# Decode attention with an MLP branch: keys loaded two heads at a time and transposed in place, output weights in three pieces

## The chip, the cores and the metric

The kernel runs on one core of one Trainium2 chip. The metric is the device time of one execution in microseconds. The kernel before takes 150.57 us (median of 3 runs, 149.56 to 151.60).

## What is computed

One token, x of 576 numbers, goes through two branches, and a scalar gate mixes them:

```python
W = 4096                                   # the last 4096 of 32768 keys
q = (x @ wq)                               # 32 query heads of 128; 16 key/value heads
scores = einsum(q, k[:, :, Sk-W:]) * 128**-0.5
o = einsum(softmax(scores), v[:, :, Sk-W:])
a = o.reshape(1, 4096) @ wo                # 4096 x 576
b = gelu(x @ w1 + b1) @ w2 + b2            # 576 -> 4608 -> 576
g = sigmoid((x * gate_w).sum())
out = g * a + (1 - g) * b
```

All inputs are bf16. The keys and the values in the window are 16.8 MB each, w1 and w2 5.3 MB each, wq and wo 4.7 MB each: 53.6 MB in all.

## The kernel before

All large loads are issued on SyncE's queue (SP) in this order: w1 (L79), wq (L83), keys, first half of w2 (L363), values, wo (L404), second half of w2 (L406). They go into four large buffers by tag, 32 KB per partition or more: w1 and key group 2 and w2 use B; wq, key group 3 and value group 2 use A; key group 0, value group 0 and value group 3 use C; key group 1, value group 1 and wo use D. SP works in program order, and a load into a buffer that is still in use holds every load behind it. So the first half of w2 waits until key group 2 has been transposed, value group 2 until key group 3 has been, value group 3 until TensorE has consumed value group 0, and wo until it has consumed value group 1.

**Keys (L287 to L316).** A group g is four heads. Partition p holds keys (p % 32) * 128 to +127 of head p // 32 of the group, `k_t[p, 128 keys, 128]`. It is loaded in two to four pieces (L280; `k_cuts`), 16 KB a partition for a 2 MB piece, 8 KB for a 1 MB piece: ten loads in all. For each half f (64 keys of each partition) two VectorE transposes (L296) work in 32x32 blocks of 4-byte words (two bf16 numbers as one word). Each takes 128x2048 words. The view `"p (n b k) -> p n k b"` on both sides makes a block's words be read, and written, with a step of 8 words (32 bytes). The result goes to `kt` (two buffers, `kt_pool`). TensorE then multiplies the half: 4 heads by 4 weight sets `qz` (L309), 16 matmuls of 512 columns into one half of `s_ps`. Its moving operand takes every second bf16 in runs of 8 (a step of 4 bytes). All 16 need both transposes. In all: 16 transposes, 128 matmuls.

**Softmax (L319 to L358).** One maximum over `s_ps` (L320), two tiny matmuls that spread it (L322, L334), eight exponentials of 128x512 on ScalarE (L347), which read `s_ps` contiguously, two VectorE transposes of 128x2048 bf16 (L355), contiguous on both sides, then the sums (L369 to L377). The first half of w2 is multiplied meanwhile (L178, L365).

**Values and output (L385 to L423).** 128 small matmuls for each of four value groups (L391), then the output scaling (L409 to L417), 64 matmuls with wo (two for each of 32 rows) and 36 with the second half of w2 (all on L178, two column halves of 288), and the output row (L425). wo comes in two loads, rows 0 to 11 and 12 to 31; the second half of w2 comes in five, the last three of 288, 144 and 144 KB.

Of the kernel before, what the change touches and what calls it, by code (L numbers as in the profile page):

```python
# [8 lines left out]
FP32 = mybir.dt.float32  # L9
BF16 = mybir.dt.bfloat16  # L10
# [6 lines left out]
def kernel(  # L17
# [15 lines left out]
    nc = tc.nc  # L33

    P = 128
    D = 576
    Hq, Hkv, Dh = 32, 16, 128
    Sk, W = 32768, 4096
    HB = 4
    NG = Hkv // HB  # L40
    NKP = P // HB
    NCK = W // NKP
    SL = NCK // 2
# [10 lines left out]
    big = ctx.enter_context(tc.tile_pool(name="big", bufs=1, side="right"))  # L54
# [42 lines left out]
    for t in range(2):  # L97
        nc.vector.tensor_copy(
            out=alt[:, t : NI + 1 : 2], in_=par[:, t : t + 1].to_broadcast([P, (NI + 1) // 2])
# [6 lines left out]
    for i in range(NI):  # L106
        nc.tensor.matmul(  # L107
            xs_ps[:, i : i + 1],
            lhsT=xdup[:, i : 2 * D : NI],
            rhs=one_b[0:1, 0:1],  # L110
            start=(i == 0),
            stop=(i == NI - 1),
            skip_group_check=True,
        )
    x2 = const.tile([P, NI, 2], BF16, name="x2")
    for t in range(2):
        nc.vector.tensor_tensor(
            out=x2[:, :, t], in0=xs_ps[:], in1=alt[:, t : t + NI], op=ALU.mult
# [13 lines left out]
        out=pen[:], in0=pen[:], scalar1=1e30, scalar2=-1e30, op0=ALU.mult, op1=ALU.add  # L132
# [3 lines left out]
    for j in range(4):  # L136
# [6 lines left out]
        out=junk_row,  # L143
# [17 lines left out]
        out=omg[:], in0=g_t[:], scalar1=-1.0, scalar2=1.0, op0=ALU.mult, op1=ALU.add  # L161
# [3 lines left out]
        out=b2g[:], in0=b2_row, scalar1=omg[0:1, 0:1], scalar2=None, op0=ALU.mult  # L165
# [3 lines left out]
        out=gh[:, 0, :], in0=hi4[:], scalar1=g_t[:, 0:1], scalar2=None, op0=ALU.mult  # L169
# [21 lines left out]
    for j in range(NJ):  # L191
        nc.tensor.matmul(
            h_ps[:, j:NF:NJ],
            lhsT=b1_t[:, j:FH:NJ],
            rhs=ident[0:2, 0:2],
            start=(j == 0),
            stop=False,
            skip_group_check=True,
# [3 lines left out]
    for i in range(NI):  # L202
        for j in range(NJ):
            nc.tensor.matmul(  # L204
                h_ps[:, j:NF:NJ],
                lhsT=w1_t[:, i, j:FH:NJ],
                rhs=x2[:, i, :],
                start=False,
                stop=(i == NI - 1 and j == NJ - 1),
                skip_group_check=True,  # L210
# [8 lines left out]
        out=poly[:],  # L219
# [20 lines left out]
    for i in range(NI):  # L240
        for j in range(Hq // 2):
            nc.tensor.matmul(  # L242
                q_ps[:, j : Hq : Hq // 2],
                lhsT=wq_t[:, i, j * Dh : (j + 1) * Dh],
                rhs=x2[:, i, :],
                start=(i == 0 and j == 0),
                stop=(i == NI - 1 and j == Hq // 2 - 1),
                skip_group_check=True,
# [4 lines left out]
    for j in range(4):  # L253
        nc.tensor.matmul(
            qj_ps[:, j, :, :].rearrange("p h t -> p (h t)"),
            lhsT=perm[:, j, :, :].rearrange("p b l -> p (b l)"),
            rhs=q_b[:],
            start=True,
            stop=True,
        )  # L260
    for b in range(4):
# [4 lines left out]
            out=diag[:, :, 0:512].rearrange("p h (j m) -> p h j m", m=P)[:, :, :, 0:2],  # L266
            in_=qj_ps[quad].rearrange("p j h t -> p h j t"),
        )
    qz = qz_flat[:, 0 : Hkv * 4 * P].rearrange("p (h j m) -> p h j m", h=Hkv, j=4)


    def head_rows(cache, g):
        src = cache[0, HB * g : HB * g + HB, Sk - W : Sk, :]
        return src.rearrange("b (k c) d -> k b (c d)", k=NKP)

    def load(tile_, cache, g, cuts):
        src = head_rows(cache, g)
        c0 = 0
        for n in cuts:
            nc.sync.dma_start(  # L280
                out=tile_[:, c0 : c0 + n, :].rearrange("p c d -> p (c d)"),
                in_=src[:, :, c0 * Dh : (c0 + n) * Dh],
            )
            c0 += n

    s_ps = ps_s.tile([P, NCK * 8], FP32, name="s_ps")
    k_cuts = ((32, 32, 64), (64, 64), (64, 64), (64, 32, 32))  # L287
    for g in range(NG):
        k_t = big.tile([P, NCK, Dh], BF16, name="k_t", tag="CDBA"[g])
        load(k_t, A_k_cache, g, k_cuts[g])  # L290
        for f in range(2):
            kt = kt_pool.tile([P, SL * Dh], BF16, name="kt", tag="kt")
            for u in range(2):
                half = SL * Dh // 2
                c0 = f * SL + u * SL // 2
                nc.vector.transpose(  # L296
                    out=kt[:, u * half : (u + 1) * half]
                    .bitcast(FP32)
                    .rearrange("p (n b k) -> p n k b", b=HB, k=8),
                    in_=k_t[:, c0 : c0 + SL // 2, :]  # L300
                    .rearrange("p c d -> p (c d)")
                    .bitcast(FP32)
                    .rearrange("p (n k b) -> p n k b", b=HB, k=8),
                )
            kv = kt[:].rearrange("p (c e b k t) -> p c e b k t", e=2, b=HB, k=8, t=2)
            for b in range(HB):
                for j in range(4):
                    h = HB * g + b
                    nc.tensor.matmul(  # L309
                        s_ps[:, f * 512 : (f + 1) * 512].rearrange("p (c k) -> p c k", k=8),  # L310
                        lhsT=qz[:, h, j, :],
                        rhs=kv[:, :, j // 2, b, :, j % 2],
                        start=(h == 0 and j == 0),
                        stop=(h == Hkv - 1 and j == 3),
                        skip_group_check=True,
                    )  # L316


    m1 = const.tile([P, 1], FP32, name="m1")  # L319
# [7 lines left out]
        out=mh4[:],  # L327
# [11 lines left out]
        out=negm[:], in0=pen[:], in1=mb_ps[:].to_broadcast([P, HB]), op=ALU.add  # L339
# [4 lines left out]
    for f in range(2):  # L344
        cs = slice(f * SL, (f + 1) * SL)
        for b in range(HB):
            nc.scalar.activation(  # L347
                out=p_t[:, cs, :, b],
                in_=s_ps[:, f * 512 : (f + 1) * 512].rearrange("p (c k) -> p c k", k=8),
                func=ACT.Exp,  # L350
                bias=negm[:, b : b + 1],
                scale=SCALE,
                accum_out=sums[:, f * HB + b : f * HB + b + 1],
            )
        nc.vector.transpose(  # L355
            out=pt[:, cs, :].rearrange("p c h -> p (c h)"),
            in_=p_t[:, cs, :, :].rearrange("p c k b -> p (c k b)"),
        )  # L358
# [5 lines left out]
    for f in range(NJ):  # L364
# [13 lines left out]
        out=rgh[:],  # L378
# [8 lines left out]
    for g in range(NG):  # L387
        v_t = big.tile([P, NCK, Dh], BF16, name="v_t", tag="CDAC"[g])
        load(v_t, A_v_cache, g, v_cuts[g])
        for c in range(NCK):  # L390
            nc.tensor.matmul(  # L391
                o_ps[:, 8 * g : 8 * g + 8, 0],
                lhsT=v_t[:, c, :],
                rhs=pt[:, c, 8 * g : 8 * g + 8],
                start=(c == 0),
                stop=(c == NCK - 1),
# [3 lines left out]
    RO = Hq * Dh // P  # L400
    wo_t = big.tile([P, RO, D], BF16, name="wo_t", tag="D")
    wo_src = A_wo.rearrange("(p r) n -> p r n", r=RO)
    for r0, r1 in ((0, 12), (12, RO)):
        nc.sync.dma_start(out=wo_t[:, r0:r1, :], in_=wo_src[:, r0:r1, :])  # L404
    for j0, j1 in ((0, 9), (9, 14), (14, 16), (16, 17), (17, 18)):
        nc.sync.dma_start(out=w2_t[:, NJ + j0 : NJ + j1, :], in_=w2_src[:, 1, j0:j1, :])  # L406
# [3 lines left out]
        out=om[:], in0=o_ps[:].to_broadcast([P, Hq, 4]), in1=rgh[:], op=ALU.mult  # L410
# [10 lines left out]
    for f in range(NJ, NF):  # L421
# [5 lines left out]
        out=out.rearrange("a b (s d) -> (a b s) d", s=2), in_=out_row[0:64:32, :]  # L427
# [31 lines left out]
```

## Time and profile before

| what | us |
|---|---|
| median of 3 runs | 150.57 |
| the profiled execution, its own time | 151.29 |
| its span in the profile | 149.5 |
| VectorE busy | 78.7 |
| TensorE busy (modelled) | 85.1 |
| DMA queue of SP: 53.61 MB, share of 16 engines' span | 85.9% |

The profile is of one execution; its span starts with the first instruction and leaves out 1.79 us of the execution's own time. "Busy" is the time in which an engine had at least one instruction running; the DMA share is the mean over 16 DMA engines. PE is TensorE, PEld its weight loads, DVE VectorE, ACT ScalarE, SPq the queue of SyncE. [...]

### The profile page before, as it was taken

What the parts mean: (1) busy time and instruction counts of PE and PEld (TensorE: products, weight loads), DVE (VectorE), ACT (ScalarE), POOL (GpSimd) and SP (SyncE); (2) the same over time, 40 slices, a digit from 0 to 9 for tenths busy, and PEclk for the clock granted to TensorE, in tenths of its full rate; (3) what the DMA queues carried; (4) which work ended last, traced back from release to release, by engine and by line L of the source; (5) the groups of instructions that cost most, each with busy time, mean ns of one, the idle gap of its engine ahead of it and who ended that gap; (6) DMA issues with size and microseconds to landing.
All of it is one profiled execution on the core that took longest, in us unless ns stands there. A gap on an engine that the chain in (4) does not pass through costs nothing.

```text
span 149.5 us, 2460 instructions
## 1 busy us (share of the span) xinstructions
PE 85.1 (57%) x1126; PEld 53.3 (36%) x1126; DVE 78.7 (53%) x81; ACT 11.9 (8%) x21; POOL 0.7 (0%) x6
## 2 busy tenths in 40 slices
PE   0189991700768188909094949550069936361791
PEld 0187991600223022404031313230069936330450
DVE  5990022099999999999999980406350000100001
ACT  3000000010000000000000000099600000000000
POOL 1000000000000000000000000000000000000000
PEclk9999999999999956999969595997555555555579
DMA  5999999999999999950089999999963899999940
GB/s 163 428 429 420 434 431 397 421 445 434 425 421 419 421 434 425 408 237 0 0 277 427 444 438 447 438 460 421 430 298 66 377 403 428 451 437 393 404 158 0
DMA packets 4344, 53.78 MB, mean 360 GB/s; under 512 B 487, under 2 KB 748, under 8 KB 1006
## 3 DMA queue, kind: packets, MB, share of 16 engines
q1 hardware_dynamic: 4324, 53.61, 85.9%
q8 instruction: 9, 0.15, 0.4%
q10 hardware_dynamic: 10, 0.01, 0.0%
q14 instruction: 1, 0.01, 0.0%
HBM read 53.62 MB, written 0.00 MB: 359 GB/s over the span
## 4 chain that ended last, share of the span: by engine, by line
DVE 38%; DMA 33%; PE 15%; ACT 7%; issue 5%; SPq 0%; DVEq 0%; ACTq 0%
DVE kt L296 34%; DMA wo_t<-in_A_wo_dram 14%; DMA wq_t<-in_A_wq_dram 14%; ACT p_t L347 6%; PE y_ps L178 5%; PE o_ps L391 5%; DMA w_t<-in_B_w_dram 4%; PE s_ps L309 4%; DVE pt L355 2%; DVE m L320 1%; PE q_ps L242 1%; PE t_ps L373 0%; DVE qz_flat L265 0%; DVE out_row L425 0%; PE mt_ps L322 0%
## 5 line engine op out<-in xcount | busy, mean ns | idle before, releaser
L296 DVE STREAM_TRANSPOSE kt<-k_t 128x2048 f32<-128x2048 f32 x16 | 58.3, 3776 | 0.0
L309 PE MATMUL s_ps<-kt,qz_flat 128*128 128x512 bf16 x128 | 38.6, 466 | 26.1 <-DVE kt L296 26.1
L309 PEld LDWEIGHTS <-qz_flat 128*128 128x128 bf16 x128 | 14.5, 113 | 49.8 <-issue 39.9
L391 PE MATMUL o_ps<-pt,v_t 128*128 128x8 bf16 x512 | 14.3, 168 | 4.6 <-issue 4.1
L391 PEld LDWEIGHTS <-v_t 128*128 128x128 bf16 x512 | 14.2, 104 | 4.8 <-issue 4.2
L347 ACT ACTIVATE p_t<-s_ps,negm 128x512 bf16<-128x512 f32 x8 | 9.7, 1425 | 66.4 <-DVE negm L338 66.4
L178 PE MATMUL y_ps<-wo_t,ov 128*1 128x288 bf16 x64 | 8.0, 443 | 6.3 <-DMA wo_t<-in_A_wo_dram 6.3
L204 PEld LDWEIGHTS <-w_t 128*128 128x128 bf16 x162 | 10.2, 165 | 1.0 <-issue 1.0
L204 PE MATMUL h_ps<-x,w_t 128*128 128x2 bf16 x162 | 10.4, 202 | 0.0
L409 DVE TENSOR_TENSOR om<-o_ps,rgh 128x128 bf16<-128x128 f32 x1 | 0.3, 291 | 18.0 <-PE o_ps L391 18.0
L425 DVE CAST out_row<-y_ps 33x288 bf16<-33x288 f32 x1 | 0.4, 449 | 16.4 <-PE y_ps L178 16.4
L355 DVE STREAM_TRANSPOSE pt<-p_t 128x2048 bf16<-128x2048 bf16 x2 | 4.6, 2311 | 7.4 <-ACT p_t L347 7.4
L178 PEld LDWEIGHTS <-ov 128*1 128x1 bf16 x64 | 4.0, 122 | 9.9 <-issue 6.3
L373 PE MATMUL t_ps<-ls,ones 128*128 128x32 f32 x2 | 0.6, 398 | 10.8 <-DVE ls L371 10.8
L242 PE MATMUL q_ps<-x,wq_t 128*128 128x2 bf16 x144 | 4.3, 166 | 4.0 <-DMA wq_t<-in_A_wq_dram 4.0
L242 PEld LDWEIGHTS <-wq_t 128*128 128x128 bf16 x144 | 4.1, 104 | 4.2 <-DMA wq_t<-in_A_wq_dram 4.2
L178 PE MATMUL y_ps<-w_t,gt 128*1 128x288 bf16 x72 | 5.3, 289 | 0.0
L213 DVE COPY hacc<-h_ps 128x36 f32<-128x36 f32 x1 | 0.2, 195 | 9.7 <-PE h_ps L204 9.7
L107 PE MATMUL xs_ps<-one_b,rows 1*128 1x1 bf16 x9 | 0.7, 195 | 6.6 <-DVE rows L104 6.6
L373 PEld LDWEIGHTS t_ps<-ls,ones 128*128 128x128 f32 x2 | 0.5, 313 | 11.1 <-issue 11.1
L320 DVE TENSOR_REDUCE m<-s_ps 128x1 f32<-128x1024 f32 x1 | 1.2, 1225 | 5.4 <-PE s_ps L309 5.4
L201 DVE MEMSET qz_flat<- 128x4240 f32 x1 | 3.6, 3592 | 0.9 <-issue 0.9
(66 smaller groups left out, 27.6 us busy)
## 6 DMA issues: line engine op xcount, KB each, us to landing
k_t<-in_A_k_cache_dram SPq DMA_DIRECT2D x6, 2048.0 KB, 31.9
v_t<-in_A_v_cache_dram SPq DMA_DIRECT2D x3, 4096.0 KB, 24.4
w_t<-in_B_w_dram SPq DMA_DIRECT2D x3, 1728.0 KB, 10.4
k_t<-in_A_k_cache_dram SPq DMA_DIRECT2D x4, 1024.0 KB
wo_t<-in_A_wo_dram SPq DMA_DIRECT2D x1, 2880.0 KB
w_t<-in_B_w_dram SPq DMA_DIRECT2D x1, 2592.0 KB
wq_t<-in_A_wq_dram SPq DMA_DIRECT2D x1, 2048.0 KB
v_t<-in_A_v_cache_dram SPq DMA_DIRECT2D x1, 2048.0 KB
```

What stands on the lines that cost most here:

```text
L107: nc.tensor.matmul(xs_ps[:, i : i + 1], lhsT=xdup[:, i : 2 * D : NI], rhs=one_b[0:1, 0:1], start=(i == 0), stop=(i == NI - 1), skip_group_ ...
L178: nc.tensor.matmul(y_ps[32 * s : 32 * s + 1, :], lhsT=vec, rhs=row[:, s * DH : (s + 1) * DH], start=start, stop=stop, skip_group_check=True,)
L201: nc.vector.memset(qz_flat[:].bitcast(FP32), 0.0)
L204: nc.tensor.matmul(h_ps[:, j:NF:NJ], lhsT=w1_t[:, i, j:FH:NJ], rhs=x2[:, i, :], start=False, stop=(i == NI - 1 and j == NJ - 1), skip_grou ...
L242: nc.tensor.matmul(q_ps[:, j : Hq : Hq // 2], lhsT=wq_t[:, i, j * Dh : (j + 1) * Dh], rhs=x2[:, i, :], start=(i == 0 and j == 0), stop=(i ...
L296: nc.vector.transpose(out=kt[:, u * half : (u + 1) * half] .bitcast(FP32) .rearrange("p (n b k) -> p n k b", b=HB, k=8), in_=k_t[:, c0 : c ...
L309: nc.tensor.matmul(s_ps[:, f * 512 : (f + 1) * 512].rearrange("p (c k) -> p c k", k=8), lhsT=qz[:, h, j, :], rhs=kv[:, :, j // 2, b, :, j ...
L320: nc.vector.reduce_max(out=m1[:], in_=s_ps[:], axis=AX.X)
L347: nc.scalar.activation(out=p_t[:, cs, :, b], in_=s_ps[:, f * 512 : (f + 1) * 512].rearrange("p (c k) -> p c k", k=8), func=ACT.Exp, bias=n ...
L355: nc.vector.transpose(out=pt[:, cs, :].rearrange("p c h -> p (c h)"), in_=p_t[:, cs, :, :].rearrange("p c k b -> p (c k b)"),)
L373: nc.tensor.matmul(t_ps[:], lhsT=ones[:], rhs=ls[:], start=True, stop=True)
L391: nc.tensor.matmul(o_ps[:, 8 * g : 8 * g + 8, 0], lhsT=v_t[:, c, :], rhs=pt[:, c, 8 * g : 8 * g + 8], start=(c == 0), stop=(c == NCK - 1),)
```

## The change

Keys are now loaded for two heads at a time. Partition p holds keys (p % 64) * 64 to +63 of head p // 64 of the pair, 16 KB a partition, one 2 MB load for a pair; the first and the last pair come in two loads of 1 MB. The loads are as many and as large as before, in the same place of SP's queue. The two transposes of a pair work on the words as they lie, with a step of one word on both sides. TensorE's moving operand now takes every fourth bf16 in runs of 16 (a step of 8 bytes), and the first 8 of a pair's 16 matmuls need only the first transpose. The keys stand in `s_ps` in another order, so an exponential takes every second fp32 of it (a step of 8 bytes), over both halves. The values are loaded as they were. wo comes in three loads, rows 0 to 11, 12 to 23 and 24 to 31.

```diff
-    k_cuts = ((32, 32, 64), (64, 64), (64, 64), (64, 32, 32))
     for g in range(NG):
-        k_t = big.tile([P, NCK, Dh], BF16, name="k_t", tag="CDBA"[g])
-        load(k_t, A_k_cache, g, k_cuts[g])
+        k_t = big.tile([P, 2, SL, Dh], BF16, name="k_t", tag="CDBA"[g])
         for f in range(2):
+            h0 = HB * g + 2 * f
+            src = A_k_cache[0, h0 : h0 + 2, Sk - W : Sk, :].rearrange(
+                "b (k c) d -> k b (c d)", k=P // 2
+            )
+            n_cut = 2 if h0 in (0, Hkv - 2) else 1
+            n = SL // n_cut
+            for u in range(n_cut):
+                nc.sync.dma_start(
+                    out=k_t[:, f, u * n : (u + 1) * n, :].rearrange("p c d -> p (c d)"),
+                    in_=src[:, :, u * n * Dh : (u + 1) * n * Dh],
+                )
             kt = kt_pool.tile([P, SL * Dh], BF16, name="kt", tag="kt")
             for u in range(2):
                 half = SL * Dh // 2
                 nc.vector.transpose(
-                    out=kt[:, u * half : (u + 1) * half]
-                    .bitcast(FP32)
-                    .rearrange("p (n b k) -> p n k b", b=HB, k=8),
-                    in_=k_t[:, c0 : c0 + SL // 2, :]
+                    out=kt[:, u * half : (u + 1) * half].bitcast(FP32),
+                    in_=k_t[:, f, u * SL // 2 : (u + 1) * SL // 2, :]
                     .rearrange("p c d -> p (c d)")
-                    .bitcast(FP32)
-                    .rearrange("p (n k b) -> p n k b", b=HB, k=8),
+                    .bitcast(FP32),
                 )
-            kv = kt[:].rearrange("p (c e b k t) -> p c e b k t", e=2, b=HB, k=8, t=2)
-            for b in range(HB):
-                for j in range(4):
...
-                        s_ps[:, f * 512 : (f + 1) * 512].rearrange("p (c k) -> p c k", k=8),
-                        rhs=kv[:, :, j // 2, b, :, j % 2],
+            kv = kt[:].rearrange("p (c e k b t) -> p c e k b t", e=2, b=2, k=16, t=2)
+            for u in range(2):
+                for b in range(2):
+                    for j in range(4):
...
+                            s_ps[:, u * 512 : (u + 1) * 512].rearrange("p (c k) -> p c k", k=16),
+                            rhs=kv[:, u * SL // 2 : (u + 1) * SL // 2, j // 2, :, b, j % 2],
...
-                in_=s_ps[:, f * 512 : (f + 1) * 512].rearrange("p (c k) -> p c k", k=8),
+                in_=s_ps[:].rearrange("p (c k u) -> p u c k", k=8, u=2)[:, f],
...
-    for r0, r1 in ((0, 12), (12, RO)):
+    for r0, r1 in ((0, 12), (12, 24), (24, RO)):
```

On TensorE, in the middle of the first 16 key matmuls, the program before reads (a name in brackets is the engine whose semaphore an instruction waits for):

```order
691 L309 MATMUL s_ps<-kt,qz_flat 128x512
692 L309 LDWEIGHTS qz_flat
693 L309 MATMUL s_ps<-kt,qz_flat 128x512
694 L309 LDWEIGHTS qz_flat
695 L309 MATMUL s_ps<-kt,qz_flat 128x512
696 L309 LDWEIGHTS qz_flat
697 L309 MATMUL s_ps<-kt,qz_flat 128x512
```

and now, at the same rows:

```order
691 L316 MATMUL s_ps<-kt,qz_flat 128x512
692 L316 LDWEIGHTS qz_flat
693 L316 MATMUL s_ps<-kt,qz_flat 128x512
694 L316 LDWEIGHTS qz_flat
695 L316 MATMUL s_ps<-kt,qz_flat 128x512 [waits DVE_49]
696 L316 LDWEIGHTS qz_flat
697 L316 MATMUL s_ps<-kt,qz_flat 128x512
```

The ninth matmul of every 16 now has a wait of its own on VectorE; before, only the first of 16 had one, for both transposes.

On SP, from the last value loads to the end, the program before reads (DMAHW0 to DMAHW7 are eight semaphores that the loads take in turn, so a load can wait for the one eight before it):

```order
20 L280 DMA v_t<-in_A_v_cache_dram 128x1x4096 x2
21 L404 DMA wo_t<-in_A_wo_dram 128x6912 [waits DMAHW6_49,PE_49]
22 L404 DMA wo_t<-in_A_wo_dram 128x11520 [waits DMAHW4_49]
23 L406 DMA w_t<-in_B_w_dram 128x5184
24 L406 DMA w_t<-in_B_w_dram 128x2880
25 L406 DMA w_t<-in_B_w_dram 128x1152 [waits DMAHW7_49]
26 L406 DMA w_t<-in_B_w_dram 128x576 [waits DMAHW0_49]
27 L406 DMA w_t<-in_B_w_dram 128x576 [waits DMAHW1_49]
```

and now:

```order
20 L281 DMA v_t<-in_A_v_cache_dram 128x1x4096 x2
21 L411 DMA wo_t<-in_A_wo_dram 128x6912 [waits DMAHW6_49,PE_49]
22 L411 DMA wo_t<-in_A_wo_dram 128x6912 [waits DMAHW4_49]
23 L411 DMA wo_t<-in_A_wo_dram 128x4608
24 L413 DMA w_t<-in_B_w_dram 128x5184
25 L413 DMA w_t<-in_B_w_dram 128x2880 [waits DMAHW7_49]
26 L413 DMA w_t<-in_B_w_dram 128x1152 [waits DMAHW0_49]
27 L413 DMA w_t<-in_B_w_dram 128x576 [waits DMAHW1_49]
28 L413 DMA w_t<-in_B_w_dram 128x576 [waits DMAHW2_49]
```

One more load stands in the queue, and each w2 load behind it takes the semaphore of the next value load: the last of them now waits for the last value load.

## Rows read from the trace of the kernel before

**Rows 1.** The page's part 2: 40 slices of 3.74 us, busy tenths.
```profile
DVE 5990022099999999999999980406350000100001
DMA  5999999999999999950089999999963899999940
```
**Rows 2.** Chain that ended last, in order of time: start us, us, what.
```profile
28.22 1.03 PE q_ps L242 x32
...
30.74 12.30 DVE kt L296 x4
...
74.58 14.47 DVE kt L296 x4
...
89.09 5.32 PE s_ps L309 x16
...
94.43 1.24 DVE m L320
...
110.48 6.82 PE o_ps L391 x256
...
146.36 0.45 DVE out_row L425
```
**Rows 3.** Waits of SP's queue: line, releaser, us in total, times, longest us.
```profile
SPq L280 <- PE o_ps L391: 20.8, 1, 20.8
...
SPq L363 <- DVE kt L296: 16.8, 1, 16.8
```
**Rows 4.** Timeline of SP's queue around two of its waits' ends.
```profile
74.56 0.34 SPq L363 DMA_DIRECT2D w_t<-in_B_w_dram  x1
...
113.91 1.83 SPq L280 DMA_DIRECT2D v_t<-in_A_v_cache_dram  x3
```
**Rows 5.** Stretches: window and us, busy PE, PEld, DVE, ACT, POOL, PEclk, DMA share, GB/s.
```profile
0.00:26.00 26.00, 15.40 (x253) 14.16 (x254) 11.25 (x49) 1.69 (x3) 0.70 (x6) 1.00 0.94 386
4.00:64.00 60.00, 37.31 (x407) 24.01 (x408) 43.00 (x59) 0.92 (x4) 0.00 (x0) 0.94 1.01 425
66.00:74.00 8.00, 3.62 (x16) 1.53 (x16) 8.00 (x3) 0.00 (x0) 0.00 (x0) 1.00 0.02 8
...
78.00:110.00 32.00, 15.77 (x79) 6.52 (x77) 17.82 (x12) 9.68 (x16) 0.00 (x0) 0.77 1.01 433
110.00:118.00 8.00, 8.00 (x290) 8.00 (x291) 0.65 (x2) 0.00 (x0) 0.00 (x0) 0.50 0.52 190
118.00:142.00 24.00, 12.72 (x281) 9.53 (x279) 0.48 (x2) 0.00 (x0) 0.00 (x0) 0.50 1.00 420
```
**Rows 6.** Groups of instructions by line and shape: busy us, mean ns | idle before.
```profile
L296 DVE STREAM_TRANSPOSE kt<-k_t 128x2048 f32<-128x2048 f32 x16 | 58.3, 3776 | 0.0
...
L347 ACT ACTIVATE p_t<-s_ps,negm 128x512 bf16<-128x512 f32 x8 | 9.7, 1425 | 66.4 <-DVE negm L338 66.4
...
L355 DVE STREAM_TRANSPOSE pt<-p_t 128x2048 bf16<-128x2048 bf16 x2 | 4.6, 2311 | 7.4 <-ACT p_t L347 7.4
```
**Rows 7.** TensorE's timeline, two groups of key matmuls.
```profile
45.57 3.62 PE L309 MATMUL s_ps<-kt,qz_flat 128*128 128x512 bf16 x16 [2.06 <-DVE kt L296]
...
89.09 5.30 PE L309 MATMUL s_ps<-kt,qz_flat 128*128 128x512 bf16 x16 [1.95 <-DVE kt L296]
```
**Rows 8.** Groups by line and shape: matmuls whose weights lie 36 bytes apart (L204) and side by side (L242).
```profile
L204 PE MATMUL h_ps<-x,w_t 128*128 128x2 bf16 x162 | 10.4, 202 | 0.0
...
L242 PE MATMUL q_ps<-x,wq_t 128*128 128x2 bf16 x144 | 4.3, 166 | 4.0 <-DMA wq_t<-in_A_wq_dram 4.0
```
**Rows 9.** TensorE's timeline, the end.
```profile
139.09 4.96 PE L178 MATMUL y_ps<-wo_t,ov 128*1 128x288 bf16 x40 [3.86 <-DMA wo_t<-in_A_wo_dram]
143.84 2.47 PE L178 MATMUL y_ps<-w_t,gt 128*1 128x288 bf16 x36
```

More of the change, by code (lines that the diff above doesn't have):

```diff
@@ L294 @@
                 half = SL * Dh // 2
-                c0 = f * SL + u * SL // 2
                 nc.vector.transpose(
-                    out=kt[:, u * half : (u + 1) * half]
-                    .bitcast(FP32)
-                    .rearrange("p (n b k) -> p n k b", b=HB, k=8),
-                    in_=k_t[:, c0 : c0 + SL // 2, :]
+                    out=kt[:, u * half : (u + 1) * half].bitcast(FP32),
+                    in_=k_t[:, f, u * SL // 2 : (u + 1) * SL // 2, :]
                     .rearrange("p c d -> p (c d)")
-                    .bitcast(FP32)
-                    .rearrange("p (n k b) -> p n k b", b=HB, k=8),
-                )
-            kv = kt[:].rearrange("p (c e b k t) -> p c e b k t", e=2, b=HB, k=8, t=2)
-            for b in range(HB):
-                for j in range(4):
-                    h = HB * g + b
-                    nc.tensor.matmul(
-                        s_ps[:, f * 512 : (f + 1) * 512].rearrange("p (c k) -> p c k", k=8),
-                        lhsT=qz[:, h, j, :],
-                        rhs=kv[:, :, j // 2, b, :, j % 2],
[L313 to L316, printed above, removed]
+                    .bitcast(FP32),
+                )
+            kv = kt[:].rearrange("p (c e k b t) -> p c e k b t", e=2, b=2, k=16, t=2)
+            for u in range(2):
+                for b in range(2):
+                    for j in range(4):
+                        h = h0 + b
+                        nc.tensor.matmul(
+                            s_ps[:, u * 512 : (u + 1) * 512].rearrange("p (c k) -> p c k", k=16),
+                            lhsT=qz[:, h, j, :],
+                            rhs=kv[:, u * SL // 2 : (u + 1) * SL // 2, j // 2, :, b, j % 2],
+                            start=(h == 0 and j == 0),
+                            stop=(h == Hkv - 1 and j == 3),
+                            skip_group_check=True,
+                        )
     m1 = const.tile([P, 1], FP32, name="m1")
```

## The prediction

> **What bounds the kernel now.** I read the 40 slices first. DMA is full from the second slice on, except for two holes: slices 18 to 21, and slices 30 and 31 [rows 1]. Through the key stage VectorE is full from 30.7 us to 89 us. The question is why the DMA stops twice, and the chain in order of time and SP's waits answer it. The chain runs through the transposes from 30.74 us until TensorE's last key matmuls start at 89.09 [rows 2]: 16 of them in 58.3 us [rows 6], 3.64 us each, with no wait. SP's longest waits name the holes: the first half of w2 waited 16.8 us for a transpose, and value group 3 waited 20.8 us for TensorE to consume value group 0 [rows 3]. Those loads went out at 74.56 and 113.91 us [rows 4]. The stretches size them: 425 GB/s while keys stream, 8 GB/s from 66 to 74 us, 433 GB/s from 78 to 110, 190 from 110 to 118, 420 after [rows 5]. So VectorE is late with the keys, and its lateness empties the DMA queue twice; everywhere else DMA sets the pace.
>
> **When bytes land.** w1 and wq are 10.03 MB; by 26 us 386 GB/s x 26 us = 10.04 MB had moved [rows 5], and the last of wq released TensorE at 28.2 [rows 2]: a landing comes about 2.1 us behind its bytes. A key pair (2.10 MB) takes 2.10/0.425 = 4.93 us. Key pieces therefore land at 30.6 and 33.0 (1 MB each), then 38.0, 42.9, 47.8, 52.8, 57.7, 62.6 (2 MB), 65.1 and 67.6 (1 MB). The change keeps sizes, row lengths and order of these loads, so I cost them at nothing.
>
> **The transposes.** Sixteen before, sixteen after, of 128x2048 words; what goes is the step of 32 bytes. No row shows a contiguous transpose of 4-byte words. The bounds: 3.64 us each, no gain, and 2.31 us, the contiguous transpose of as many bf16 [rows 6]. Cheaper than that has no row, and since DMA paces the stage below 4.93/2 = 2.46 us, it would bring nothing. I take 2.31, the row equal in form and element count. Two take 4.62 us a pair, less than the 4.93 us in which a pair arrives, so VectorE waits for data: the pairs end at 35.3, 42.6, 47.5, 52.4, 57.4, 62.3 and 67.2, the last pair's halves at 69.5 and 71.8 (against 89.05).
>
> **TensorE in the key stage.** Still 128 matmuls of 512 columns. A group of 16 took 3.62 us, or 5.30 us when it began at the lower clock [rows 7]: 0.226 us each at best. The new step of 8 bytes has no row. [...] The upper bound comes from weight loads: with columns 36 bytes apart a pair of weight load and matmul took 10.4/162 = 64 ns, side by side 4.3/144 = 30 ns [rows 8], a factor of 2.15, so 0.486 us a matmul. I take no cost, because two neighbours 8 bytes apart are nearer to 4 than to 36. Then a pair costs 3.6 us of its 4.93, with pauses under 2 us. After the last transpose 8 matmuls remain instead of 16: 1.8 us, end at 73.6 (against 94.41).
>
> [...]
>
> **Softmax.** From the end of the scores to the first value matmul took 110.48 - 94.41 = 16.1 us [rows 2]; now it would be 73.6 + 16.1 = 89.7. The exponentials read `s_ps` with a step of 8 bytes; nothing before does, and I bound each of the eight (9.7/8 = 1.21 us apart [rows 6]) by no cost and by twice as long, 9.7 us in all. I take none, because the sum hardly feels it (below).
>
> **DMA after the keys.** The first half of w2 can go out at 62.3 instead of 74.56, before the last key bytes have moved at 66 us, so the first hole closes. w2's half and value groups 0 to 2 are 2.65 + 12.58 = 15.24 MB, 35.2 us at 433 GB/s: until 101.2. Value group 3 needs group 0 consumed: 89.7 + 3.4 (half of the 6.82 us of rows 2) = 93.1. That is some 7 us before the queue runs dry (a load's first bytes move about 1 us behind its issue), so the second hole closes too, and this margin is what covers the exponentials. The added wait of the last w2 piece for the last value piece (landed about 113) costs nothing: behind it stands only the output, and it is wanted near 128. Value group 3 takes 4.19/0.433 = 9.7 us, wo and w2's second half 7.37 MB/0.420 = 17.5 us. Last bytes at 101.2 + 9.7 + 17.5 = 128.4.
>
> **The tail.** Before, the last bytes moved at 139.1 - 2.1 + 2.65/0.420 = 143.3 (the last wo landed at 139.1, and w2's 2.65 MB follow it). TensorE began the last 40 wo matmuls at 139.09 (0.119 us each) and ended the 36 of w2 at 146.3 [rows 9], 3.0 us behind the bytes. With three pieces 24 of the 40 are done earlier and 16 remain, 1.9 us; then the last small w2 pieces decide, 2.1 us behind the bytes, and some matmuls: 2.4 us (it could be 2.1 to 3.0). The output takes 149.5 - 146.34 = 3.16 us as before.
>
> **Sum.** 128.4 + 2.4 + 3.16 = 134.0 us of span, plus the 1.79 us around it: 135.8 us, against 151.29 of the same execution before (15.5 less: 14.9 from the two holes, 0.6 from the tail). Against the median of 150.57 the same gain would give 135.1.
>
> **The rivals.**
>
> *TensorE becomes the bound, 146.0.* If the new step doubles a matmul to 0.452 us, the stage ends at 33.0 + 128 x 0.452 = 90.9. The pair whose transposes release w2 waits for its `kt` buffer until 33.0 + 64 x 0.452 = 61.9 and ends at 66.5, so DMA pauses 1.5 us; value group 0 is consumed at 90.9 + 16.1 + 3.4 = 110.4 and group 3 starts 8.7 us late. 135.8 + 10.2 = 146.0. For it: the weight loads' factor. [...] Part of it (up to 0.3 us a matmul) would cost almost nothing.
>
> *The exponentials double, 138.3.* Value group 0 is consumed 9.7 us later, at 102.8; group 3's bytes begin 2.6 us late, at 103.8. Then 135.8 + 2.5 = 138.3. Nothing in the profile speaks for or against, as all its reads of `s_ps` are contiguous. [...]
>
> *The transposes stay at 3.64 us, 148.0.* That is so if words of 4 bytes are slow in themselves, not their step; the two transposes of rows 6 differ in both. Only the shorter ends remain: 8 matmuls instead of 16 (half of 5.30 = 2.7 us, which move group 3's start) and 0.6 in the tail. 151.3 - 3.3 = 148.0.
>
> *Slower: the matmul's step costs more than doubling.* Place: the key matmuls. The point from which it decides: group 0 must be consumed later than 113.9 as now, so 33.0 + 128c + 19.5 > 113.9, c = 0.48 us. The weight loads' factor (0.486) reaches just there. At 0.55 us the group is consumed at 122.9, 9 us later: 151.3 + 9 - 0.6 = 159.7. Against it: that would be worse per column than loads that skip 36 bytes.
>
> **How the numbers follow.** Forecast 0.64, with a range of its own of 133 to 138 (DMA at 433 GB/s to the end, or a tail and a start that are 2 us worse); TensorE as the bound 0.20; exponentials 0.06; unchanged transposes 0.07; slower 0.03. A measurement of this kernel can tell about 2% from no change. Faster: 0.64 + 0.20 + 0.06 and half of the unchanged transposes, which lie on the edge: 0.93. Within 2%: 0.04. Slower: 0.03. The range runs from 133 to 145 us: it takes in the forecast, the doubled exponentials and most of TensorE's slowing, short of full doubling.
>
> **What would show it.** Right: transposes near 2.3 us with waits for key loads before each pair; groups of 8 key matmuls near 1.8 us; scores done near 74 us; no DMA slice under 9 tenths from the second to the last but two; w2's first half issued near 62 us. Wrong: transposes of 3.6 us (the step was not the cause), key matmuls over 0.3 us apart without a wait, an SP wait of value group 3 on TensorE that leaves the DMA empty, or a lower DMA rate in the key stage, for which nothing here speaks.

## The result, and the profile after

The changed kernel takes 145.78 us (median of 4 runs, 145.26 to 145.91) against 150.12 us for the kernel before (median of 4 too): a ratio of 0.969 with a 95% interval of 0.961 to 0.977. It is faster, as forecast, but by 4.3 us and not by 15; the forecast of 135.8 and its range (to 145.0) both miss. The time is that of the rival in which TensorE becomes the bound, 146.0. (Ratios here and below leave out runs over 1.5% slower than the fastest of the same kernel, so one can differ from the quotient of the medians beside it.)

Two things in the description ahead have to be put right. First, the loads have the key block outside the head ("k b (c d)"): before, partition p holds 128 keys of head p % 4; after, it holds 64 keys of head p % 2. Heads alternate from partition to partition. That is why a transposed block of 32 words mixes heads, why the old transposes moved words about, and why the new matmuls step over the other head's words. Second, the old transposes stepped on the writing side alone: the view `"p (n b k) -> p n k b"` stands on `kt`, and the view of `k_t` is `"p (n k b) -> p n k b"`, the words as they lie. No time in the prediction depends on either, but experiment 5 does.

The page's part 2 of the changed kernel, 40 slices of 3.60 us (PEclk is the clock that TensorE was granted, here in tenths of the full one, in the stretches and in [rows 5] as a share of it):

```profile
PE   0189992718999999999999997740099764384391
DVE  5991003068489858393939102205710000100001
...
PEclk9999999999999999999999999867555555559959
DMA  5999999999999999997999999999404999999930
```

VectorE, full from 30.7 to 89 us before [rows 1], now has pauses. TensorE is full instead, from 40 to 89 us, at a granted clock of 1.00. Of the DMA's first hole a dip is left, in slice 19; the second hole is still there, in slices 29 to 31.

The groups of instructions that answer to [rows 6] and [rows 7] (busy us, mean ns of one | idle before, releaser):

```profile
L316 PE MATMUL s_ps<-kt,qz_flat 128*128 128x512 bf16 x128 | 55.6, 609 | 3.6 <-DVE kt L305 3.6
L305 DVE STREAM_TRANSPOSE kt<-k_t 128x2048 f32<-128x2048 f32 x16 | 36.2, 2294 | 12.8 <-PE s_ps L316 9.2
...
L354 ACT ACTIVATE p_t<-s_ps,negm 128x512 bf16<-128x512 f32 x8 | 9.7, 1411 | 60.9 <-DVE negm L345 60.9
```

The transposes take 2.29 us instead of 3.78, as forecast, and now wait 9.2 us for TensorE to free `kt`; the exponentials take the same 9.7 us with their new step. The matmuls have grown. The chain that ended last, in order of time, says how much (start us, us, what):

```profile
37.97 2.32 DVE kt L305
...
40.34 48.52 PE s_ps L316 x112
...
88.88 1.24 DVE m L327
...
104.92 6.82 PE o_ps L398 x256
...
136.61 4.06 PE y_ps L178 x36
...
140.69 0.45 DVE out_row L432
```

112 matmuls run back to back for 48.5 us: 0.433 us each, against 0.226 in [rows 7]. The scores are done at 88.9 instead of 94.4, and that is all that is left of the 21 us by which they were to come sooner. The waits of SP's queue (us in total, times, longest) show what follows, against [rows 3]:

```profile
SPq L281 <- PE o_ps L398: 23.8, 1, 23.8
...
SPq L370 <- DVE kt L305: 8.2, 1, 8.2
```

The first half of w2 waits only 8.2 us for its transpose, but value group 3 waits longer than before for value group 0 to be consumed. The loads go out at these times (compare [rows 4]), and the stretches give the price (window and us, busy PE, PEld, DVE, ACT, POOL, PEclk, DMA share, GB/s):

```profile
65.79 0.34 SPq L370 DMA_DIRECT2D w_t<-in_B_w_dram  x1
...
108.35 1.83 SPq L281 DMA_DIRECT2D v_t<-in_A_v_cache_dram  x3
```

```profile
63.00:66.00 3.00, 3.00 (x8) 0.80 (x7) 2.76 (x2) 0.00 (x0) 0.00 (x0) 1.00 0.84 350
66.00:70.00 4.00, 4.00 (x10) 1.03 (x9) 1.84 (x1) 0.00 (x0) 0.00 (x0) 1.00 0.87 289
66.00:101.00 35.00, 27.15 (x93) 8.12 (x91) 13.20 (x9) 9.17 (x15) 0.00 (x0) 0.93 1.00 421
101.00:118.00 17.00, 11.46 (x410) 11.43 (x411) 3.25 (x5) 0.51 (x2) 0.00 (x0) 0.50 0.56 228
```

From 63 to 70 us the DMA falls short of 421 GB/s by (1 - 350/421) x 3 + (1 - 289/421) x 4 = 1.8 us: that is left of the first hole, as the first half of w2 goes out at 65.8. From 101 to 118 it moves 228 GB/s: (1 - 228/421) x 17 = 7.8 us lost, because value group 3 may not be loaded before 108.4.

### The profile page after: what moved, and what is told of

Its sections match the earlier page's. It is cut to its first block, busy times and chain, and to the rows that moved or that the text cites. A ratio compares the mean times of both kernels' runs of the same rounds, so it can differ in the third digit from the quotient of the medians.

```text
span 143.9 us, 2461 instructions
## 1 busy us (share of the span) xinstructions
PE 102.9 (72%) x1126; PEld 53.9 (37%) x1126; DVE 56.5 (39%) x81; ACT 11.9 (8%) x21; POOL 0.7 (0%) x6
## 4 chain that ended last, share of the span: by engine, by line
PE 42%; DMA 41%; ACT 7%; DVE 5%; SPq 2%; issue 1%; ACTq 0%
PE s_ps L316 34%; DMA w_t<-in_B_w_dram 21%; DMA k_t<-in_A_k_cache_dram 20%; ACT p_t L354 7%; PE o_ps L398 5%; PE y_ps L178 3%; DVE kt L305 2%; DVE pt L362 2%; SPq L411 1%; DVE m L327 1%; SPq L298 1%; PE t_ps L380 0%; DVE out_row L432 0%; PE mt_ps L329 0%; PE mb_ps L341 0%
## 5 line engine op out<-in xcount | busy, mean ns | idle before, releaser
L316 PE MATMUL s_ps<-kt,qz_flat 128*128 128x512 bf16 x128 | 55.6, 609 | 3.6 <-DVE kt L305 3.6
L305 DVE STREAM_TRANSPOSE kt<-k_t 128x2048 f32<-128x2048 f32 x16 | 36.2, 2294 | 12.8 <-PE s_ps L316 9.2
L316 PEld LDWEIGHTS <-qz_flat 128*128 128x128 bf16 x128 | 14.7, 115 | 43.6 <-issue 42.3
L354 ACT ACTIVATE p_t<-s_ps,negm 128x512 bf16<-128x512 f32 x8 | 9.7, 1411 | 60.9 <-DVE negm L345 60.9
L204 PEld LDWEIGHTS <-w_t 128*128 128x128 bf16 x162 | 10.2, 165 | 1.0 <-issue 1.0
L204 PE MATMUL h_ps<-x,w_t 128*128 128x2 bf16 x162 | 10.4, 202 | 0.0
L178 PE MATMUL y_ps<-wo_t,ov 128*1 128x288 bf16 x64 | 5.8, 344 | 4.8 <-DMA wo_t<-in_A_wo_dram 4.8
L178 PE MATMUL y_ps<-w_t,gt 128*1 128x288 bf16 x72 | 7.7, 396 | 2.0 <-DMA w_t<-in_B_w_dram 2.0
L242 PE MATMUL q_ps<-x,wq_t 128*128 128x2 bf16 x144 | 4.3, 166 | 3.8 <-DMA wq_t<-in_A_wq_dram 3.8
L178 PEld LDWEIGHTS <-gt 128*1 128x1 bf16 x72 | 4.2, 111 | 5.0 <-issue 2.2
L178 PEld LDWEIGHTS <-ov 128*1 128x1 bf16 x64 | 3.2, 97 | 7.1 <-issue 4.9
L242 PEld LDWEIGHTS <-wq_t 128*128 128x128 bf16 x144 | 4.1, 104 | 4.0 <-DMA wq_t<-in_A_wq_dram 4.0
```

The costliest lines, as they stand in the source:

```text
L178: nc.tensor.matmul(y_ps[32 * s : 32 * s + 1, :], lhsT=vec, rhs=row[:, s * DH : (s + 1) * DH], start=start, stop=stop, skip_group_check=True,)
L204: nc.tensor.matmul(h_ps[:, j:NF:NJ], lhsT=w1_t[:, i, j:FH:NJ], rhs=x2[:, i, :], start=False, stop=(i == NI - 1 and j == NJ - 1), skip_grou ...
L242: nc.tensor.matmul(q_ps[:, j : Hq : Hq // 2], lhsT=wq_t[:, i, j * Dh : (j + 1) * Dh], rhs=x2[:, i, :], start=(i == 0 and j == 0), stop=(i ...
L305: nc.vector.transpose(out=kt[:, u * half : (u + 1) * half].bitcast(FP32), in_=k_t[:, f, u * SL // 2 : (u + 1) * SL // 2, :] .rearrange("p ...
L316: nc.tensor.matmul(s_ps[:, u * 512 : (u + 1) * 512].rearrange("p (c k) -> p c k", k=16), lhsT=qz[:, h, j, :], rhs=kv[:, u * SL // 2 : (u + ...
L354: nc.scalar.activation(out=p_t[:, cs, :, b], in_=s_ps[:].rearrange("p (c k u) -> p u c k", k=8, u=2)[:, f], func=ACT.Exp, bias=negm[:, b : ...
```

## The experiments

**1. The step of TensorE's reads alone.** In the changed kernel the moving operand is taken from words side by side instead of every second word.

```diff
-            kv = kt[:].rearrange("p (c e k b t) -> p c e k b t", e=2, b=2, k=16, t=2)
+            kv = kt[:].rearrange("p (c e b k t) -> p c e b k t", e=2, b=2, k=16, t=2)
-                            rhs=kv[:, u * SL // 2 : (u + 1) * SL // 2, j // 2, :, b, j % 2],
+                            rhs=kv[:, u * SL // 2 : (u + 1) * SL // 2, j // 2, b, :, j % 2],
```

> The changed kernel with the moving operand of the key matmuls taken in a step of 4 bytes instead of 8; the rows multiplied are then the wrong keys, everything else (loads, transposes, number and order of matmuls, waits) stays. Theory (the step of 8 bytes alone doubled the matmuls): 0.22 to 0.23 us a matmul instead of 0.433, a group of 8 in 1.8 us, scores done near 74 us instead of 88.9, no hole in the DMA, 136 us (135 to 137.5). Rival (the doubling comes from the rest of the new order: waits after every 8 matmuls, the alternating halves of s_ps, runs of 16, or VectorE writing kt without a step beside it): still 0.43 us a matmul and 145.8 us.

Measured: 135.96 us, ratio to before 0.910 (0.902 to 0.919). On TensorE's timeline each group of 8 now waits for its transpose:

```profile
60.08 1.90 PE L316 MATMUL s_ps<-kt,qz_flat 128*128 128x512 bf16 x8 [0.82 <-DVE kt L305]
...
71.56 1.89 PE L316 MATMUL s_ps<-kt,qz_flat 128*128 128x512 bf16 x8 [0.30 <-DVE kt L305]
```

and the stretches that had the holes are full:

```profile
63.00:66.00 3.00, 2.18 (x11) 0.88 (x10) 3.00 (x2) 0.00 (x0) 0.00 (x0) 1.00 1.04 434
66.00:70.00 4.00, 3.40 (x16) 1.34 (x14) 4.00 (x3) 0.00 (x0) 0.00 (x0) 1.00 1.00 426
101.00:118.00 17.00, 8.77 (x267) 7.92 (x269) 0.48 (x2) 0.00 (x0) 0.00 (x0) 0.50 1.01 419
```

A group of 8 takes 1.9 us, scores end at 73.4, and both holes are gone. Nothing but the step was changed, so the step of 8 bytes alone is the doubling, and the doubling alone is the 9.8 us between 145.78 and 135.96; the 1.8 and 7.8 us of the two holes account for 9.6 of them. The rival, that the rest of the new order had slowed TensorE, falls.

**2. Which steps cost how much.** The 16 matmuls of each key pair read `kt` in a plain step; the eight pairs have eight steps.

```diff
-                            rhs=kv[:, u * SL // 2 : (u + 1) * SL // 2, j // 2, :, b, j % 2],
+                            rhs=kt[:, 0 : 512 * s : s],   # s = 4, 1, 2, 3, 4, 6, 8, 16 (of 2 bytes) for pairs 0 to 7
```

> The changed kernel with the 16 matmuls of each key pair reading kt in a plain step of its own: 8 bytes for the first pair, then 2, 4, 6, 8, 12, 16 and 32 bytes for the other seven (the numbers are then meaningless, the count and size of the matmuls as they were). Theory A (a fixed rate of 8-byte reads: one column per two clocks once two columns do not share 8 bytes): 2 and 4 bytes at 0.22 us, 6 bytes in between, 8 bytes and all above at 0.43. Theory B (16-byte lines, the cost grows until every column has a line of its own): 8 bytes at 0.43 and 16 and 32 bytes clearly above, 0.6 us or more. Theory C (only short runs cost): 8 bytes in one long run at 0.22 us.

Measured on TensorE's timeline (pairs 1 to 7, steps of 2, 4, 6, 8, 12, 16 and 32 bytes, in this order):

```profile
40.34 3.61 PE L322 MATMUL s_ps<-kt,qz_flat 128*128 128x512 bf16 x16
45.37 3.76 PE L324 MATMUL s_ps<-kt,qz_flat 128*128 128x512 bf16 x16 [1.42 <-DVE kt L305]
50.27 5.60 PE L326 MATMUL s_ps<-kt,qz_flat 128*128 128x512 bf16 x16 [1.14 <-DVE kt L305]
55.70 7.40 PE L328 MATMUL s_ps<-kt,qz_flat 128*128 128x512 bf16 x16
62.92 11.00 PE L330 MATMUL s_ps<-kt,qz_flat 128*128 128x512 bf16 x16
73.74 14.58 PE L332 MATMUL s_ps<-kt,qz_flat 128*128 128x512 bf16 x16
88.14 14.87 PE L334 MATMUL s_ps<-kt,qz_flat 128*128 128x512 bf16 x16
```

From the start of one group to the next without a wait between: 8 bytes (62.92 - 55.70)/16 = 0.451 us a matmul, 12 bytes 0.676, 16 bytes 0.900, and 32 bytes no more than 16. Theory A (flat from 8 bytes) and theory C (a long run is free) fall; the growth of theory B up to 16 bytes holds. But the longest steps were read at another clock, as the stretches show (PEclk before the DMA share):

```profile
63.00:66.00 3.00, 3.00 (x6) 0.50 (x5) 2.86 (x2) 0.00 (x0) 0.00 (x0) 1.00 1.04 431
66.00:70.00 4.00, 4.00 (x7) 0.74 (x6) 1.64 (x1) 0.00 (x0) 0.00 (x0) 0.60 1.03 438
70.00:73.60 3.60, 3.60 (x6) 0.62 (x5) 0.00 (x0) 0.00 (x0) 0.00 (x0) 0.50 1.08 462
```

The clock fell at about 66.8 us (0.60 is the mean from 66 to 70, 0.50 what follows), in the middle of the group with 12 bytes, after TensorE had been busy without a pause since 50.3.

**3. The long steps at the full clock.** As before it, but the first 12 of 16 matmuls read without a step, and only the last 4 with one.

```diff
+                        if n_mm <= 12:
+                            nc.tensor.matmul(so, rhs=kt[:, 0 : 512], **kw)
+                        else:   # s = 2, 4, 3, 6, 8, 12, 16, 4 for pairs 0 to 7
+                            nc.tensor.matmul(so, rhs=kt[:, 0 : 512 * s : s], **kw)
```

> The run with a step of its own for each key pair once more, with the first 12 of each 16 matmuls reading kt without a step and only the last 4 with one: 4, 8, 6, 12, 16, 24, 32 and again 8 bytes for the eight pairs (the numbers are meaningless), so that the long steps too run at the full granted clock. Theory (a line of 16 bytes takes 1.76 ns whatever the clock, a column at least 0.43 ns): 0.22 us at 4 bytes, 0.34 at 6, 0.45 at 8, 0.68 at 12, 0.90 at 16, 24 and 32. [...]

Measured, the groups of 4 (L331: 16 bytes, L335: 32 bytes) between groups without a step (L321), and the granted clock (the figure before the DMA share) of the two stretches:

```profile
58.28 3.76 PE L331 MATMUL s_ps<-kt,qz_flat 128*128 128x512 bf16 x4
61.87 2.77 PE L321 MATMUL s_ps<-kt,qz_flat 128*128 128x512 bf16 x12
...
72.17 3.83 PE L335 MATMUL s_ps<-kt,qz_flat 128*128 128x512 bf16 x4
75.82 2.77 PE L321 MATMUL s_ps<-kt,qz_flat 128*128 128x512 bf16 x12
```

```profile
58.30:61.80 3.50, 3.50 (x5) 0.44 (x4) 3.50 (x2) 0.00 (x0) 0.00 (x0) 1.00 0.99 417
72.20:75.80 3.60, 3.60 (x5) 0.42 (x4) 0.55 (x1) 0.00 (x0) 0.00 (x0) 1.00 1.06 454
```

(61.87 - 58.28)/4 = 0.90 us at 16 bytes and (75.82 - 72.17)/4 = 0.91 at 32, at clock 1.00: the same as at 0.50. So the cost of the long steps is not the clock's. Per column it is 0.44 ns up to 4 bytes (3.61 us/16/512 in experiment 2), then about 0.11 ns for each byte of step, and 1.76 ns (0.90 us/512) from 16 bytes on. My estimate from these times: every 16 bytes that are touched take 1.76 ns.

**4. Half of the matmuls slow.** The first 8 of 16 keep the step of 8 bytes, the second 8 have 4.

```diff
-                            rhs=kv[:, u * SL // 2 : (u + 1) * SL // 2, j // 2, :, b, j % 2],
+                            rhs=(kv[:, u * SL // 2 : (u + 1) * SL // 2, j // 2, :, b, j % 2] if u == 0
+                                 else kw[:, u * SL // 2 : (u + 1) * SL // 2, j // 2, b, :, j % 2]),
```

> The changed kernel with the step of 4 bytes in the second 8 of each 16 key matmuls only (those multiply the wrong keys); the first 8 keep the step of 8 bytes. A pair then costs TensorE 8 x 0.433 + 8 x 0.226 = 5.3 us against 4.9 us in which its data arrive: scores done near 77 us, about 4 us later than with the step of 4 bytes throughout. Theory (the lateness costs only what goes beyond the margin before value group 3 is wanted, about 6 us): 136 us as with the step of 4 bytes throughout, no hole in the DMA. Rival (the time follows the matmuls in proportion): half of the 9.8 us between the two kernels, 141 us.

Measured: 135.93 us, ratio to before 0.908 (0.899 to 0.917). TensorE's timeline and two stretches:

```profile
40.40 37.55 PE L317 MATMUL s_ps<-kt,qz_flat 128*128 128x512 bf16 x112 [1.97 <-DVE kt L305]
```

```profile
66.00:101.00 35.00, 21.46 (x303) 12.15 (x301) 13.12 (x13) 9.68 (x16) 0.00 (x0) 0.80 1.01 432
101.00:118.00 17.00, 9.54 (x302) 8.78 (x303) 0.48 (x2) 0.00 (x0) 0.00 (x0) 0.50 0.99 416
```

TensorE is the bound of the key stage here too (112 matmuls without a wait, scores done at 78.0, 4.5 us later than in experiment 1), and the whole costs nothing: the DMA stays full. So it matters only how far the stage goes past the margin of value group 3, as the prediction had it, and not that TensorE bounds the stage.

**5. Which side of a transpose feels the step.** On the kernel of experiment 1, four forms of the transpose, two key pairs each.

```diff
-                    out=kt[:, u * half : (u + 1) * half].bitcast(FP32),
-                    in_=k_t[:, f, u * SL // 2 : (u + 1) * SL // 2, :]
+                    # cin, cout: words as they lie; pin, pout: a step of 32 bytes (kernel before: pout, cin)
+                    # pairs 0-1: out=cout, in_=cin; 2-3: out=cout, in_=pin; 4-5: out=pout, in_=cin; 6-7: out=pout, in_=pin
```

> The kernel with the step of 4 bytes on TensorE and four forms of the transpose, one for two key pairs each: no step on either side, a step of 32 bytes on the reading side only, on the writing side only, on both (the words are then in other places; counts and sizes as they were). Theory (each word in another place costs the side that steps, and the two costs overlap): 2.3, about 3.6, about 3.6 and 3.77 us. Rival 1 (only writes feel the step): 2.3, 2.3, 3.7, 3.77. Rival 2 (the costs add): 2.3, 3.0, 3.0, 3.77.

Measured (L312 no step, L314 reading side, L316 writing side, L318 both):

```profile
L318 DVE STREAM_TRANSPOSE kt<-k_t 128x2048 f32<-128x2048 f32 x4 | 15.0, 3835 | 0.0
L314 DVE STREAM_TRANSPOSE kt<-k_t 128x2048 f32<-128x2048 f32 x4 | 14.8, 3766 | 0.5 <-DMA k_t<-in_A_k_cache_dram 0.5
L316 DVE STREAM_TRANSPOSE kt<-k_t 128x2048 f32<-128x2048 f32 x4 | 14.6, 3768 | 0.0
L312 DVE STREAM_TRANSPOSE kt<-k_t 128x2048 f32<-128x2048 f32 x4 | 9.1, 2301 | 2.7 <-DMA k_t<-in_A_k_cache_dram 2.6
```

A step on either side alone costs 3.77 us, on both 3.84. The kernel before has the form of L316, a step on the writing side alone, and its 3.78 us [rows 6] agree; the form with both is not its form, as its expectation took it to be. Moving the step from the writing to the reading side would have saved nothing: it has to go from both.

**6. wo in three loads, alone.** The kernel before with that one line changed.

```diff
-    for r0, r1 in ((0, 12), (12, RO)):
+    for r0, r1 in ((0, 12), (12, 24), (24, RO)):
```

> The kernel before with wo in three loads, the only change. Theory of the prediction: 24 of the last 40 wo matmuls are done earlier, the end comes 0.6 us sooner, 149.5 (-0.4%). Rival: the tail is set by how fast TensorE goes through its last matmuls at the clock it is granted there, and breaking its work up keeps the clock down: no gain or up to 1.5 us worse.

Measured: 150.53 us beside 151.04 for before, ratio 1.007 (1.002 to 1.011). Medians and ratio point opposite ways, and the runs of either kernel scatter (149.13 to 151.09, and 148.53 to 151.81), so they can't tell a gain of 0.6 us from none. TensorE's end, against [rows 9]:

```profile
136.34 4.75 PE L178 MATMUL y_ps<-wo_t,ov 128*1 128x288 bf16 x40 [1.29 <-DMA wo_t<-in_A_wo_dram]
142.28 1.27 PE L178 MATMUL y_ps<-w_t,gt 128*1 128x288 bf16 x18 [1.19 <-DMA w_t<-in_B_w_dram]
144.07 1.73 PE L178 MATMUL y_ps<-w_t,gt 128*1 128x288 bf16 x18 [0.52 <-DMA w_t<-in_B_w_dram]
```

The wo matmuls do end earlier, at 141.1 instead of 143.8, but TensorE then waits twice for w2 (1.19 and 0.52 us) and ends at 145.8 instead of 146.3, 0.5 us sooner in this pair of traces. In this trace the w2 loads set the end.

**7. A kernel that has both.** If each head is spread over all 128 partitions (32 keys each), a transposed block belongs to one head: no regrouping is needed, and the matmul reads every second bf16 as in the kernel before. Rows of the loads become 8 KB, the loads stay 2 MB.

```diff
-                "b (k c) d -> k b (c d)", k=P // 2
+                "b (k c) d -> k b (c d)", k=P
...
-            kv = kt[:].rearrange("p (c e k b t) -> p c e k b t", e=2, b=2, k=16, t=2)
+            kv = kt[:].rearrange("p (b c e k t) -> p b c e k t", b=2, e=2, k=32, t=2)
...
+                            s_ps[:, v * 512 : (v + 1) * 512].rearrange("p (c k) -> p c k", k=32),
+                            rhs=kv[:, b, v * 16 : (v + 1) * 16, j // 2, :, j % 2],
...
-                in_=s_ps[:].rearrange("p (c k u) -> p u c k", k=8, u=2)[:, f],
+                in_=s_ps[:].rearrange("p (c k u) -> p u c k", k=8, u=4)[:, 2 * f : 2 * f + 2],
```

> A whole kernel that has both the transposes without a step and a moving operand with a step of 4 bytes: each head is spread over all 128 partitions (32 keys each, 8 KB a partition), so a transposed block of 32 words belongs to one head. Loads stay 2 MB (two heads in 8 KB rows), the exponentials read s_ps with a step of 16 bytes. Theory: the same as with the step of 4 bytes alone, transposes 2.31 us, matmuls 0.22 to 0.23 us, 136 us (135 to 137.5). Rival 1 (rows of 8 KB stream slower): under 415 GB/s in the key stage and 1 to 3 us more. Rival 2 (the exponentials feel the step of 16 bytes): more than 1.21 us each, and time only if the values wait for them.

Measured: 136.44 us, ratio to before 0.912 (0.903 to 0.921). Its groups, and its key stage:

```profile
L302 DVE STREAM_TRANSPOSE kt<-k_t 128x2048 f32<-128x2048 f32 x16 | 36.0, 2290 | 5.4 <-DMA k_t<-in_A_k_cache_dram 5.2
L313 PE MATMUL s_ps<-kt,qz_flat 128*128 128x512 bf16 x128 | 32.7, 400 | 11.6 <-DVE kt L302 11.6
...
L351 ACT ACTIVATE p_t<-s_ps,negm 128x512 bf16<-128x512 f32 x8 | 9.7, 1415 | 46.1 <-DVE negm L342 46.1
```

```profile
4.00:64.00 60.00, 42.69 (x437) 26.54 (x438) 37.58 (x62) 0.92 (x4) 0.00 (x0) 1.00 1.01 421
```

It beats both kernels. VectorE now waits for loads and TensorE for VectorE; rows of 8 KB stream at 421 GB/s against 425, a difference too small to tell; the exponentials don't feel a step of 16 bytes either (1415 ns against 1425 in [rows 6]).

**8. The same kernel with wo in two loads, and once more with three**, on one chip.

```diff
-    for r0, r1 in ((0, 12), (12, 24), (24, RO)):
+    for r0, r1 in ((0, 12), (12, RO)):
```

> The kernel with one head over 128 partitions, but with wo in two loads as before. Theory: 40 instead of 16 wo matmuls stand behind the last wo load; they and the 36 of w2 end 0.9 us later if the clock rises in between as it did in the kernel before, up to 2.5 us later if it does not: 137.3 to 139. Rival (the tail's end is set by the last w2 load alone): the same time as with three loads.

> The kernel with one head over 128 partitions and wo in three loads once more, on the same chip as the one with two loads: 136.4 us as in its first run, within 0.7.

Measured: 136.33 us with two loads and 136.48 with three, ratios to before 0.911 (0.906 to 0.917) and 0.912 (0.906 to 0.919). TensorE's end with two loads:

```profile
124.33 4.29 PE L178 MATMUL y_ps<-wo_t,ov 128*1 128x288 bf16 x40 [3.84 <-DMA wo_t<-in_A_wo_dram]
128.45 2.56 PE L178 MATMUL y_ps<-w_t,gt 128*1 128x288 bf16 x36
```

and with three:

```profile
121.62 4.70 PE L178 MATMUL y_ps<-wo_t,ov 128*1 128x288 bf16 x40 [1.11 <-DMA wo_t<-in_A_wo_dram]
127.57 3.53 PE L178 MATMUL y_ps<-w_t,gt 128*1 128x288 bf16 x36 [1.25 <-DMA w_t<-in_B_w_dram]
```

With two loads the 36 w2 matmuls come late but in a row with what stands before them, and take 2.56 us; with three they begin earlier, behind a wait, and take 3.53. The ends are 131.0 and 131.1. The granted clock differs as the times do: 1.00 while the 36 ran with two loads, 0.65 with three (and 0.63 in the trace of experiment 7, where they took 3.67 us from 127.66). That the clock alone takes the head start away isn't shown. The forecast of 0.9 to 2.5 us falls.

The trace with three loads shows one thing more. Its granted clock was 0.65 from 40.5 to 77.1 us, where the trace of experiment 7 has 1.00: 112 key matmuls ran without a wait in 36.62 us, 0.327 each. The execution took 136.10 us, no more than the others of its kernel, so a slower TensorE cost nothing here either, as in experiment 4.

## Why the prediction was right or wrong

**What bounds the kernel: right.** VectorE's lateness made both holes. With transposes and matmuls that keep up (experiment 1) both close, and the time is 135.96 where the sum gave 135.8. Its parts hold too: scores at 73.4 (73.6 forecast), last y matmul at 131.06 (130.8), span 134.3 (134.0). In the tail only the size held: not the last small w2 pieces decided, but TensorE's 36 matmuls with w2, which ran from 127.02 without a wait and took 4.04 us at a granted clock of 0.58. That their end lay 2.7 us behind the 128.4 worked out for the last bytes, and so near the term of 2.4, is luck.

**The transposes: right.** The step of 32 bytes was the cost, on one side alone (experiment 5). 2.31 us was taken from the transpose of bf16; 2.29 was measured, 4.50 us for the two of a pair. The rival of unchanged transposes is out.

**TensorE in the key stage: this step failed.** It read: "I take no cost, because two neighbours 8 bytes apart are nearer to 4 than to 36." Measured were 0.433 us a matmul instead of 0.226. Nearness in bytes was no argument: the upper bound lay a factor of 2.15 above no cost, the row with 36 bytes pointed to that factor, and the cost already begins beyond 4 bytes (experiments 2 and 3: 6 bytes (55.70 - 50.27)/16 = 0.339 us). The factor of 2.15 came near the 1.92 measured at 8 bytes, but it was no upper bound for this operand: at 16 bytes the factor is 4 (0.90 against 0.226). The chance of 0.20 was too low for a cost on which 10 us hung, and the range should have reached the full doubling at 146.0 that the text itself had worked out.

**The rival that came true.** Its mechanism was right in every link: TensorE back to back, transposes waiting for `kt` (9.2 us), the first half of w2 later than forecast (65.8 us; 66.5 worked out), value group 3 held until 108.4 (110.4 worked out). It put 1.5 us on the first hole and 8.7 on the second; 1.8 and 7.8 were measured. At 0.433 us instead of 0.452 the scores end 2 us sooner than it said, which makes the second hole shorter; the last y matmul ends at 140.67 where 130.8 + 10.2 = 141.0 was worked out. "Part of it (up to 0.3 us a matmul) would cost almost nothing" is shown by experiment 4, at a mean of 37.55/112 = 0.335 us.

**The exponentials: right to take none.** 9.7 us for eight with a step of 8 bytes and of 16 bytes (1411 and 1415 ns against 1425).

**wo in three loads: the 0.6 us are not shown.** The wo matmuls do end earlier, but that gain is spent in another way than the text said: TensorE waits for the first and second piece of w2, not for the last small ones (experiment 6), or goes through its w2 matmuls at a lower clock (experiment 8). One pair of traces ends 0.5 us sooner and one doesn't, and neither pair of runs shows a gain. Since 0.6 is less than a run can tell, it doesn't matter for the verdict.

## What to carry to other kernels

When a regrouping is taken off one engine, whoever reads next may have to pay for it: price the next reader's access pattern from a row with a step, and where the only rows are far apart, let the range reach the farther one. Look first for a layout in which nobody regroups: here, spreading one head over all partitions does it, and takes 9% off where the change took 3%. And the cost of a stage that gets a new bound is only what goes past the next load's margin: with the matmuls at 0.335 us it was nothing, at 0.433 it was 9.8 us.

## What the runs showed of the hardware that was not expected

- TensorE's moving operand (bf16, 512 columns) takes 0.23 us a matmul in steps of 2 and 4 bytes (3.61 and 3.76 us for 16), 0.34 at 6 bytes, 0.43 to 0.45 at 8, 0.68 at 12, 0.90 at 16, 0.91 at 32. For 16 bytes it was 0.90 us at a granted clock of 1.00 and of 0.50 alike.
- In the run with a step of its own for each pair the granted clock fell from 1.00 to 0.50 at about 66.8 us, although TensorE had no pause; it was reading with a step of 12 bytes. In two traces of the kernel of experiment 7 the clock of the key stage was 1.00 in one and 0.65 in the other, with spans of 134.5 and 134.3 us. What decides it isn't shown.
- A VectorE transpose of 4-byte words costs 3.77 us with a step of 32 bytes on the reading or on the writing side, hardly more (3.84) with one on both, and 2.30 us without.
